# Fused attention and two feed-forward stages: the order of the first stage's tiles and block products on TensorE

## The chip, the cores and the metric

The kernel runs on one core of one Trainium2 chip. The metric is the device time of one execution in microseconds, the median over the runs shown. TensorE (PE) does the matrix products, its weight loads are a separate row (PEld), VectorE (DVE) and ScalarE (ACT) do elementwise work and are the only ones besides PE that reach PSUM here, GpSimd (POOL) and SyncE (SP) issue DMAs.

## What is computed

Banded attention over 2 batches of 8 heads, 576 positions of 64; its output is a matrix x of 1152 tokens by 512. Two feed-forward stages follow:

```python
p = domain_probs / (domain_probs.sum(-1, keepdims=True) + 1e-09)
for e in range(4):                          # w1[e]: 512 x 1024, w2[e]: 1024 x 512
    out += p[:, e:e + 1] * (np.maximum(x @ w1[e], 0.0) @ w2[e])
h = out @ w_in                              # 512 x 2048
g = (a0 + a1*h + a2*h*h + a3*h*h*h) / (1 + |b0|*|h| + |b1|*h*h + 1e-06)
return g @ w_out                            # 2048 x 512
```

The change is in the first of the two, the experts.

## The kernel before

**Tiling.** Tokens are cut into three chunks c of 384 and nine output tiles t of 128 (tile t lies in chunk t // 3). The 4096 hidden columns of the four experts are 16 units u of 256, and two units make a group g (expert g // 2), so there are eight groups. Every fp32 operand is split into a high and a low part, and a product of two such operands is three matmuls (high by high, high by low, low by high).

**Three kinds of work on PE.** `h_paced` (line 894) makes the hidden values of one unit for one chunk: 24 matmuls of 384 columns into a PSUM tile `ps_h` of two banks, then a Relu on ACT that writes the high part `hh` (line 481) and a DVE instruction for the low part `hl` (line 485). `strassen` (line 917) makes them for chunks 1 and 2 together, with seven block products in place of eight; each `product` is six matmuls of 384 columns (line 933). `o_paced` (line 904) makes an output tile of a group: twelve matmuls of 512 columns into a bank `ps_o` (line 509), which ACT scales into `part` (line 539) and POOL adds to `acc` in SBUF by an accumulating DMA (line 540). Products and hidden values are the 384-column work, output tiles the 512-column work.

**A block of seven products** holds two `ps_h` tiles. In `yz` the bank y is written by products 1, 6, 7 and 4, and z by product 2; in `vz` the bank v is written by 5 and 3, and q holds a sum. Product 1 goes to y, and ACT copies y to z (line 947). Product 6 (called with `s(0, 0), t_(0)`) adds to y, product 5 starts v, and ACT copies v to the SBUF tile `p5` (line 955). Then DVE writes v = y + p5 (line 956). Product 7 adds to y, and DVE writes q = y + p5 (line 940, in `add`). Product 2 adds to z, product 3 to v, product 4 to y. Relus of both tiles end the block.

**The order** is fixed in Python: `tc.manual_schedule()` keeps each engine's instructions as they are written. `later(wait, ...)` puts a DVE or ACT step into the program behind the first PE step that passes its due time, so the second add of a block (`add(q, y, p5)`) stands behind product 2. `settle(key)` forces pending steps of that name into the program. Weight splits, sums of weight blocks and a conversion of the second stage's weights fill DVE in between. Waits between engines are set by the framework from the tiles that instructions read and write.

**Output tiles among the rest.** The loop over groups (line 987) hands each `strassen` call three fills, one output tile each, run behind products 1, 5 and 2 (`then(0)` to `then(2)`). Two more places between the hidden values of chunk 0 take one tile and two. Tiles 0 to 2 of a group are done in its second block, the other six in the next group. `o_bank` rotates over two PSUM banks; `h_tile` rotates over three two-bank tiles.

Of the kernel before, what the change touches and what calls it, by code (L numbers as in the profile page):

```python
# [18 lines left out]
F32 = mybir.dt.float32  # L19
# [82 lines left out]
def body(ctx, tc, qkv, mask, dp, w1, w2, w1d, w2d, coef, out):  # L102
# [51 lines left out]
    def block_sums(raw):  # L154

        r = raw.rearrange("p (h k i f) -> p h i k f", h=2, k=2, i=2)
        a11, a12, a21, a22 = r[:, 0, 0], r[:, 1, 0], r[:, 0, 1], r[:, 1, 1]
        sums = (
            (a22, a21, a22, ALU.add), (a21, a11, a21, ALU.subtract),
            (a11, a22, a11, ALU.subtract), (a12, a12, a11, ALU.subtract),  # L160
        )
# [316 lines left out]

    def relu_parts(u, c, ps):
        def high():  # L480
            nc.scalar.activation(new_h(u, c)[0], ps[:, :, :TC], AF.Relu)  # L481
# [137 lines left out]
    with tc.manual_schedule():  # L619
# [271 lines left out]
                    then()  # L891
            behind(0.0, key, act_then(key, act, dve, COST["token"]))

        def h_paced(u, c):
            settle(("w1", u))
            ps = h_tile()
# [20 lines left out]
        def strassen(u, between_):  # L917

            for k in (("w1", u), ("sw", u, 0), ("sw", u, 1), "tokens"):
                if k != ("sw", u, 0) or u % 2 == 0:  # L920
                    if u > 2 or k[0] != "sw":
                        settle(k)
            yz, vz = h_tile(), h_tile()
            z, y, v, q = yz[:, 0, :TC], yz[:, 1, :TC], vz[:, 0, :TC], vz[:, 1, :TC]
            w = [i.rearrange("p (h k i f) -> p h i k f", h=2, k=2, i=2) for i in (w1s[u][:, 0], w1s[u][:, 1])]
            block = lambda m, h, i: [t[:, h, i] for t in m]
            x = lambda c, h: [t[:, 2 * h:2 * h + 2] for t in xt[c]]
            t_ = lambda n: [t[:, n] for t in tt]
            s = lambda h, i: [sw[u, i][:, n, h] for n in range(2)]
            def product(out, a, b, first=False):  # L930
# [8 lines left out]
            def add(out, a, b):  # L939
                later(0.2, COST["add"], ("add", u), lambda: nc.vector.tensor_tensor(out=out, in0=a, in1=b, op=ALU.add))  # L940

            def then(n):
                for f, *args in between_[n]:
                    f(*args)

            product(y, block(w, 0, 0), x(1, 0), first=True)
            nc.scalar.copy(z, y)
            then(0)
            settle(("sw", u, 0))
            product(y, s(0, 0), t_(0))  # L950
            settle("first")
            settle(("sw", u, 1))
            product(v, s(1, 1), x(2, 0), first=True)
            p5 = st.tile([128, TC], F32, tag="p5", name="p5")
            nc.scalar.copy(p5, v)
            later(0.8, COST["add"], ("add", u), lambda: nc.vector.tensor_tensor(out=v, in0=y, in1=p5, op=ALU.add))
            then(1)
            settle(("add", u))
            settle("second")
            product(y, s(0, 1), t_(1))  # L960
            add(q, y, p5)
            product(z, block(w, 1, 0), x(1, 1))
            then(2)
            settle(("add", u))
            product(v, s(1, 0), x(2, 1))
            settle("third")
            product(y, block(w, 1, 1), t_(2))
            for c, ps, wait in ((1, yz, 1.1), (2, vz, 2.0)):
                high, low = relu_parts(u, c, ps)
                high()  # L970
                later(wait, COST["relu"], ("h", u, c), low)

        def loads(*us):
            for load, u in us:
# [12 lines left out]
        for g in range(NG1):  # L987
# [3 lines left out]
            if g == 0:  # L991
                later(0.0, COST["osum"], ("o", 0, 3), lambda: o_sum(0, 3, ps_2[3]))
                token_sums()
                tokens_later(temp[0], *(t[:, 0] for t in tt))
                sums_later(2)
                sums_split_later(2, 0)
# [5 lines left out]
                sums_split_later(2, 1)  # L1002
# [4 lines left out]
            if g in BLOCKED:  # L1007
                if g > 1:
                    h_paced(u, 0)
                sums_split_later(u + 1, 1)  # L1010
                if g > 1:
                    split_later(w2s, "w2", u + 1)
                if again:
                    split_later(w1s, "w1", u + 2)
                if g > 1:
                    o_paced(g - 1, 6)
                    h_paced(u + 1, 0)
                if g > 1:
                    o_paced(g - 1, 7)
                    if again:  # L1020
                        o_paced(g - 1, 8)
                fills = [o((g - 1, j if g > 1 else j + 3)) for j in (3, 4, 5)]
                w2_loads = (load_w2, u + 2), (load_w2, u + 3)
                free = [(load_w1, u + 3)] * (g > 1) + [w2_loads[0]] * (g == 1) + [w2_loads[1]]
                free = [(weights_free, *free)] if again else []
                fills[2].insert(0, (sums_split_later, u + 1, 0, free))
                strassen(u, fills)
# [7 lines left out]
                strassen(u + 1, (o((g, 0)), o((g, 1)), o((g, 2) if again else (g - 1, 8))))  # L1035
                if g == 1:
                    Window.spare[:] = [None, lone[:, 0], lone[:, 1]]
                if again:
                    sums_split_later(u + 2, 0, [(loads, (load_w1, u + 4))])
                    sums_later(u + 3)  # L1040
                else:
                    loads(*w2_loads, (load_w1, u + 4), (load_w1, u + 5))

        while Pace.prep:
            run_prep()
# [8 lines left out]
        early_open, late = tc.tile_pool(name="early", bufs=1), []  # L1054
        early = early_open.__enter__()
        dt = [rat.tile([128, 3, 2, TC], F32R, tag=f"t{i}", name=f"t{i}", bufs=1) for i in range(2)]
        ps_h, ps_2, p5s, x2_ps, turned, copied, rational = {}, {}, {}, {}, set(), {}, {}
        tokens = lambda c, h: [t[:, 2 * h:2 * h + 2] for t in xt[c]]

# [81 lines left out]
        def product(n, u):  # L1141
# [3 lines left out]
            if n == 5:  # L1145
# [12 lines left out]
                5: lambda: (place(2, 0), summed(1, 1), tokens(2, 0)),  # L1158
                6: lambda: (place(1, 1), summed(0, 0), d(0)),
                7: lambda: (place(1, 1), summed(0, 1), d(1)),  # L1160
            }[n]()
            first = n in (1, 5)
            for k in range(2):
# [145 lines left out]
```

## Time and profile before

| | |
|---|---|
| median of 3 runs | 631.29 us (631.0 to 631.78) |
| profiled execution, its own time | 631.96 us |
| its span, first to last instruction | 630.2 us |
| PE busy | 622.2 us, 99% of the span |
| DVE, ACT, POOL busy | 522.8, 370.4, 87.7 us |
| granted TensorE clock | 1.000 (2.4 GHz) |
| chain that ended last | PE 97% |

Busy PE time overlaps itself, since matmuls are pipelined: two rows of 0.33 us stand 0.17 us apart. So the time of PE's work is read from starts, not from durations. The experts' stretch runs from about 110 to 413 us.

### The profile page before, as it was taken

The page shows a single profiled execution, that of the slowest core. Times are in us where ns is not written, and L with a number is a line of the kernel's source. Part 1 is how long each engine was busy: PE and PEld are TensorE (multiplying, and loading weights), DVE is VectorE, ACT ScalarE, POOL GpSimd, SP SyncE. Part 2 cuts the span into 40 slices and gives each one's busy share as a digit, 9 for nine tenths or more (in the row PEclk, how much of TensorE's full clock was granted, in tenths as well). Part 3 has the DMA queues.
Part 4 walks back from the last instruction along what each step waited for, and adds up shares of the span by engine and source line. Part 5 has one row for each costly group of instructions (what it writes and reads, how often), then busy time and mean ns, then how long its engine had stood idle before and what let it go on. Part 6 is the DMA issues. An engine that isn't in the chain of part 4 may idle for free.

```text
span 630.2 us, 9848 instructions
## 1 busy us (share of the span) xinstructions
PE 622.2 (99%) x3726; PEld 555.8 (88%) x3728; DVE 522.8 (83%) x788; ACT 370.4 (59%) x682; POOL 87.7 (14%) x103
## 2 busy tenths in 40 slices
PE   8999999999999999999999999999999999999997
PEld 5888898999999999998998999888998889899886
DVE  7687488898888888889798888549898999899894
ACT  6787624345545554554555554336688686887760
POOL 2223230012112112101102112000000011111100
PEclk9999999999999999999999999999999999999999
DMA  9945302269869869869869877681231563573333
GB/s 284 316 136 185 103 20 68 100 166 241 246 187 270 245 180 258 257 186 267 241 182 261 236 220 219 209 323 48 88 133 56 190 201 89 116 235 52 66 81 103
DMA packets 39535, 111.28 MB, mean 177 GB/s; under 512 B 4256, under 2 KB 5024, under 8 KB 37440
## 3 DMA queue, kind: packets, MB, share of 16 engines
q1 hardware_dynamic: 29104, 92.14, 43.2%
q0 software_dynamic: 9936, 18.09, 16.5%
q8 instruction: 29, 0.48, 0.3%
q10 hardware_dynamic: 448, 0.43, 0.3%
q14 instruction: 18, 0.15, 0.1%
HBM read 67.13 MB, written 25.43 MB: 147 GB/s over the span
## 4 chain that ended last, share of the span: by engine, by line
PE 97%; DVE 1%; ACT 1%; issue 0%; POOL 0%; POOLq 0%
PE ps_o L509 46%; PE ps_h L464 21%; PE ps_h L933 16%; PE ps_h L1165 7%; PE ps_v L428 2%; PE ps_s L414 1%; PE ps_h L509 1%; PE ps_s L359 1%; PE ps_h L651 1%; PE ps_h L1099 1%; ACT pr L393 0%; POOL pr L403 0%; PE ps L359 0%; DVE xl L889 0%; DVE hl L485 0%
## 5 line engine op out<-in xcount | busy, mean ns | idle before, releaser
L509 PE MATMUL ps_o<-w,hh 128*128 128x512 f32 (+1 forms) x848 | 229.5, 392 | 0.3 <-DVE xl L452 0.3
L509 PEld LDWEIGHTS ps_o<-w,hh 128*128 128x128 f32 x848 | 156.6, 188 | 28.4 <-DVE xl L452 0.7
L509 PE MATMUL ps_o<-w,hl 128*128 128x512 f32 (+1 forms) x424 | 131.4, 391 | 0.1
L464 PE MATMUL ps_h<-xh,w 128*128 128x384 f32 x464 | 125.2, 338 | 0.0
L509 PEld LDWEIGHTS ps_o<-w,hl 128*128 128x128 f32 x424 | 79.3, 188 | 18.0 <-DVE hl L485 0.6
L464 PEld LDWEIGHTS ps_h<-xh,w 128*128 128x128 f32 x464 | 84.4, 188 | 2.3 <-issue 1.2
L540 POOL DMA_DIRECT2D acc<-part x51 | 44.7, 876 | 275.7 <-ACT part L539 216.9
L539 ACT ACTIVATE part<-ps_o,p_sb 128x512 f32<-128x512 f32 x51 | 35.1, 689 | 78.5 <-PE ps_o L509 36.8
L464 PE MATMUL ps_h<-xl,w 128*128 128x384 f32 x232 | 77.6, 335 | 0.0
L481 ACT ACTIVATE hh<-ps_h 128x768 fp32r<-128x768 f32 x48 | 37.4, 810 | 34.6 <-PE ps_h L464 23.0
L485 DVE SCALAR_TENSOR_TENSOR hl<-ps_h,hh 128x768 fp32r<-128x768 f32 x48 | 44.5, 950 | 10.8 <-ACT hh L481 10.7
L464 PEld LDWEIGHTS ps_h<-xl,w 128*128 128x128 f32 x232 | 43.6, 188 | 0.6
L1084 POOL DMA_DIRECT2D acc<-part x18 | 15.6, 867 | 184.3 <-ACT part L1083 183.8
L933 PE MATMUL ps_h<-t,sw 128*128 128x384 f32 x168 | 34.3, 339 | 0.0
L829 DVE TENSOR_TENSOR w<-raw,w 128x512 fp32r<-128x512 f32 x48 | 32.8, 684 | 1.0 <-ACT w L825 0.9
L393 ACT ACTIVATE pr<-pr,mx 128x80 f32<-128x80 f32 (+1 forms) x84 | 29.8, 358 | 6.1 <-DVE mx L387 4.7
L933 PE MATMUL ps_h<-xh,sw 128*128 128x384 f32 x112 | 33.2, 337 | 0.0
L268 ACT ACTIVATE x<-x 128x512 f32<-128x512 f32 x32 | 21.8, 681 | 18.1 <-DVE t L265 12.3
L933 PEld LDWEIGHTS ps_h<-t,sw 128*128 128x128 f32 x168 | 30.3, 188 | 2.2
L576 DVE SCALAR_TENSOR_TENSOR sq<-sq,absb,ab 128x768 f32<-128x768 f32 x24 | 24.2, 1013 | 7.9 <-ACT sq L565 6.7
L933 PE MATMUL ps_h<-xh,w 128*128 128x384 f32 x104 | 30.7, 335 | 0.0
L825 ACT CAST w<-raw 128x512 fp32r<-128x512 f32 x48 | 28.0, 617 | 0.0
(157 smaller groups left out, 1120.0 us busy)
## 6 DMA issues: line engine op xcount, KB each, us to landing
acc<-part POOLq DMA_DIRECT2D x69, 256.0 KB, 4.4
raw<-in_w_dram SPq DMA_DIRECT2D x32, 512.0 KB, 5.0
w<-w SPq DMA_DIRECT2D x14, 1024.0 KB, 6.3
w<-lone SPq DMA_DIRECT2D x19, 512.0 KB, 4.2
x<-in_w1d_dram SPq DMA_DIRECT2D x16, 512.0 KB, 3.8
x<-in_w2d_dram SPq DMA_DIRECT2D x16, 512.0 KB, 5.0
w<-w SPq DMA_DIRECT2D x13, 512.0 KB, 4.4
sw<-sw SPq DMA_DIRECT2D x12, 512.0 KB, 7.5
```

Source lines behind the costliest of these rows:

```text
L393: nc.scalar.activation(pr[:, j, i], pr[:, j, i], AF.Exp, scale=-1.0, bias=self.mx[:, j, i:i + 1], accum_out=self.total[:, j, i:i + 1],)
L464: nc.tensor.matmul(ps[:, i, :TC], lhsT=a[:, k, f], rhs=b[:, k], start=k + n == 0, stop=k + n == 5,)
L481: nc.scalar.activation(new_h(u, c)[0], ps[:, :, :TC], AF.Relu)
L485: nc.vector.scalar_tensor_tensor(out=hl, in0=ps[:, :, :TC], scalar=0.0, in1=hh.bitcast(F32), op0=ALU.max, op1=ALU.subtract,)
L509: nc.tensor.matmul(ps, lhsT=a[:, i, tk], rhs=b[:, i, cols], start=v + n == 0, stop=v + n == 6)
L539: nc.scalar.activation(part, ps, AF.Copy, scale=pe)
L540: nc.gpsimd.dma_start(acc[t], part, accum_op=ALU.add)
L576: nc.vector.scalar_tensor_tensor(out=self.sq, in0=self.sq, scalar=absb[:, 1:2], in1=self.ab, op0=ALU.mult, op1=ALU.add,)
L825: nc.scalar.copy(store[u][:, 0, s_], raws[nm, u][:, s_])
L829: nc.vector.tensor_tensor(out=w[:, 1, s_], in0=raws[nm, u][:, s_], in1=w[:, 0, s_].bitcast(F32), op=ALU.subtract)
L933: nc.tensor.matmul(out, lhsT=a[i][:, k], rhs=b[j][:, k], start=first and k + n == 0, stop=k + n == 3, skip_group_check=not first,)
L1165: nc.tensor.matmul(out, lhsT=a[i][:, k], rhs=b[j][:, k], start=first and k + m == 0, stop=k + m == 3, skip_group_check=not first,)
```

## The change

The number of matmuls and of instructions on every other engine stays the same (DVE 784, ACT 601, SP 177, POOL 97 in both programs). The seven products become methods of a class `Blocks`, and the loop calls them in a new order: block `a` (first unit of the group) and block `b` (second) now overlap, and output tiles stand in three runs of three tiles per group (6 to 8 and 3 to 5 of the group before, 0 to 2 of its own). Product 5 is written to a bank of the output tiles and copied to `p5` from there, so a `vz` tile is taken only at the first sum. `h_tile` can be told whether to take the third tile. The sums of weight blocks are formed in another order, and the products' halves are renamed to suit; the second stage gets the same renaming. The third tile of some runs has its `part` step held back by 1.5 us.

```diff
-    def h_tile(count=[0]):
+    count = [0]
+    def h_tile(last=None):
         count[0] += 1
-        pool = third[0] if third and count[0] % 3 == 0 else psh
+        last = third and count[0] % 3 == 0 if last is None else last
+        pool = third[0] if last else psh
...
-        def o_paced(g, t):
+        def o_paced(g, t, wait=0.0):
...
             if by_dma(g, t):
-                o_sum(g, t, ps)
+                if wait:
+                    later(wait, 0.0, ("o", g, t), lambda: o_sum(g, t, ps))
+                else:
+                    o_sum(g, t, ps)
...
+            def add(self, n, wait=0.2):
+                out, y, p5 = self.place(n), self.place(1), self.p5
+                later(
+                    wait, COST["add"], ("add", self.u),
+                    lambda: nc.vector.tensor_tensor(out=out, in0=y, in1=p5, op=ALU.add),
+                )
...
+            def fifth(self):
+                settle("first")
+                ps = o_bank()[:, :TC]
+                self.product(ps, self.summed(0, 1), self.x(2, 0), first=True)
+                self.p5 = st.tile([128, TC], F32, tag="p5", name="p5")
+                nc.scalar.copy(self.p5, ps)
...
+            def seventh(self):
+                settle(("add", self.u))
+                self.product(self.place(1), self.summed(0, 0), self.t(1))
+                self.add(3)
+
+            def second(self):
+                self.product(self.place(0), self.plain(1, 0), self.x(1, 1))
+
+            def third(self):
+                settle(("add", self.u))
+                self.product(self.place(2), self.summed(1, 0), self.x(2, 1))
...
+                h_paced(u, 0, False)
...
+                run(g - 1, 6, 7, 8)
+                a.first(False)
+                h_paced(u + 1, 0, True)
+                a.fifth()
+                a.sixth()
+                a.sum_up(0.2, False)
+                run(g - 1, 3, 4)
+                sums_split_later(u + 1, 0, free)
+                o_paced(g - 1, 5, 1.5)
+                a.seventh()
+                a.second()
+            b.first(True)
+            a.third()
+            a.fourth()
+            next_sums()
+            b.fifth()
+            b.sixth()
+            b.sum_up(0.2, False)
+            run(g, *range(3 if again else 2))
+            b.seventh()
+            b.second()
+            b.third()
+            b.fourth()
```

Before, on PE, in the second block of group 3: the end of product 2 (adds to `ps_h_2354`, the block's `yz`), one output tile `ps_o_2447`, and the start of product 3 (adds to `ps_h_2355`, its `vz`):

```order
L933 MATMUL ps_h_2354<-xh1_119,w1_1996 128x384 x2
L933 MATMUL ps_h_2354<-xl1_120,w1_1996 128x384
L933 MATMUL ps_h_2354<-xh1_119,w1_1996 128x384
L509 MATMUL ps_o_2447<-w2_1971,hh_2083 128x512 [waits Activation_49]
L509 MATMUL ps_o_2447<-w2_1971,hh_2083 128x512 x3
L509 MATMUL ps_o_2447<-w2_1971,hl_2084 128x512 x2
L509 MATMUL ps_o_2447<-w2_2128,hh_2151 128x512 x4
L509 MATMUL ps_o_2447<-w2_2128,hl_2152 128x512 x2
L933 MATMUL ps_h_2355<-xh2_121,sw_2313 128x384 [waits DVE_49]
L933 MATMUL ps_h_2355<-xl2_122,sw_2313 128x384
```

Now, the same place, `yz` being `ps_h_2331` and `vz` `ps_h_2383`:

```order
L935 MATMUL ps_h_2331<-xh1_119,w1_2012 128x384 x2
L935 MATMUL ps_h_2331<-xl1_120,w1_2012 128x384
L935 MATMUL ps_h_2331<-xh1_119,w1_2012 128x384
L935 MATMUL ps_h_2383<-xh2_121,sw_2302 128x384 [waits DVE_49]
L935 MATMUL ps_h_2383<-xl2_122,sw_2302 128x384
L935 MATMUL ps_h_2383<-xh2_121,sw_2302 128x384 x2
L935 MATMUL ps_h_2383<-xl2_122,sw_2302 128x384
L935 MATMUL ps_h_2383<-xh2_121,sw_2302 128x384
```

Product 3 still waits for DVE, and the output tile that stood between products 2 and 3 is gone from there.

The DVE rows of that place now (`ps_h_2383<-ps_h_2331,p5` is the block's second add, and it waits for PE and for nothing else; in the program before, its row reads the same):

```order
L833 TENSOR_TENSOR w2_2425<-raw_2171,w2_2425 128x512
L285 TENSOR_SCALAR f_2455<-t_2430 128x512 [waits DVE_49]
L289 SCALAR_TENSOR_TENSOR f_2455<-x64_2299,f_2455 128x512 [waits DVE_49]
L961 TENSOR_TENSOR ps_h_2383<-ps_h_2331,p5_2374 128x384 [waits PE_49]
L833 TENSOR_TENSOR w1_2457<-raw_2310,w1_2457 128x512 [waits DMAHW3_49,Activation_49]
L298 TENSOR_TENSOR f_2455<-f_2455,t_2430 128x512 [waits DVE_49]
L311 SCALAR_TENSOR_TENSOR f_2455<-x64_2299,f_2455 128x512 [waits DVE_49]
L489 SCALAR_TENSOR_TENSOR hl_2488<-ps_h_2383,hh_2487 128x768 [waits Activation_49]
```

Between the add and the low part of the Relu (`hl`, L489) stand three instructions of weight work. In the two programs product 3 has a DVE wait, and this add is the last DVE instruction ahead of it that writes its tile.

Now, in the first block of group 3 (`yz` is `ps_h_2162`, `vz` `ps_h_2237`): the end of product 2, product 1 of the second block (into `ps_h_2331`), and product 3 of the first:

```order
L935 MATMUL ps_h_2162<-xh1_119,w1_1762 128x384
L935 MATMUL ps_h_2331<-xh1_119,w1_2012 128x384 [waits PE_49]
L935 MATMUL ps_h_2331<-xl1_120,w1_2012 128x384
L935 MATMUL ps_h_2331<-xh1_119,w1_2012 128x384 x2
L935 MATMUL ps_h_2331<-xl1_120,w1_2012 128x384
L935 MATMUL ps_h_2331<-xh1_119,w1_2012 128x384
L935 MATMUL ps_h_2237<-xh2_121,sw_2083 128x384 [waits DVE_49]
```

Before, an output tile stood there as in the second block; now one product of the other block does.

Counted in the two orders from output tile 4 of group 0 to the last tile of group 7, PE changes from products to output tiles 55 times before and 23 times now, with 726 matmuls of 512 columns and 870 of 384 in both.

## Rows read from the trace of the kernel before

**Rows 1.** The page: busy time of each engine, and the granted clock in 40 slices.

```profile
PE 622.2 (99%) x3726; PEld 555.8 (88%) x3728; DVE 522.8 (83%) x788; ACT 370.4 (59%) x682; POOL 87.7 (14%) x103
...
PEclk9999999999999999999999999999999999999999
```

**Rows 2.** PE's two longest waits: line, releaser, us in total, times, longest.

```profile
PE ps_h L651 <- DVE warm L641: 1.2, 1, 1.2
PE ps_s L414 <- POOL pr L403: 1.0, 1, 1.0
```

**Rows 3.** Two stretches of 48 us, by engine: busy us (x count), clock, DMA share, GB/s.

```profile
141.00:189.00 48.00, 48.00 (x243) 43.45 (x242) 41.37 (x72) 25.58 (x43) 7.80 (x9) 1.00 0.81 224
189.00:237.00 48.00, 48.00 (x242) 43.45 (x241) 41.98 (x74) 26.30 (x45) 7.82 (x9) 1.00 0.82 234
```

**Rows 4.** PE in time, two output tiles between products: start us, us, instruction, count.

```profile
231.01 1.09 PE L509 MATMUL ps_o<-w,hh 128*128 128x512 f32 x4
...
233.78 1.07 PE L509 MATMUL ps_o<-w,hh 128*128 128x512 f32 x4
...
236.50 0.33 PE L933 MATMUL ps_h<-xh,w 128*128 128x384 f32 x1
...
237.56 0.39 PE L509 MATMUL ps_o<-w,hh 128*128 128x512 f32 x1
```

**Rows 5.** PE in time, second block of group 3, from product 7 to product 4.

```profile
212.94 1.23 PE L933 MATMUL ps_h<-t,sw 128*128 128x384 f32 x6
...
214.87 0.33 PE L933 MATMUL ps_h<-xh,w 128*128 128x384 f32 x1
215.04 1.08 PE L509 MATMUL ps_o<-w,hh 128*128 128x512 f32 x4
...
217.80 0.33 PE L933 MATMUL ps_h<-xh,sw 128*128 128x384 f32 x1
...
218.87 1.20 PE L933 MATMUL ps_h<-t,w 128*128 128x384 f32 x6
219.91 0.33 PE L464 MATMUL ps_h<-xh,w 128*128 128x384 f32 x1
```

**Rows 6.** DVE in time: second adds (L940) of the second blocks of groups 2 and 3.

```profile
167.34 0.57 DVE L940 TENSOR_TENSOR ps_h<-ps_h,p 128x384 f32<-128x384 f32 x1 [1.41 <-PE ps_h L933]
...
215.24 0.57 DVE L940 TENSOR_TENSOR ps_h<-ps_h,p 128x384 f32<-128x384 f32 x1 [0.95 <-PE ps_h L933]
215.71 0.68 DVE L829 TENSOR_TENSOR w<-raw,w 128x512 fp32r<-128x512 f32 x1
```

**Rows 7.** All second adds (L940): count, ns min/median/max, first and last start; idle before.

```profile
L940 DVE TENSOR_TENSOR ps_h<-ps_h,p x14: 566/567/567, 103.8 to 404.1; 128x384 f32<-128x384 f32 x14
...
  PE ps_h L933: 17.0, 13
```

**Rows 8.** DVE, PEld and PE in time, where PE waited for a DVE result.

```profile
95.07 0.95 DVE L485 SCALAR_TENSOR_TENSOR hl<-ps_h,hh 128x768 fp32r<-128x768 f32 x1
...
96.07 0.30 PEld L509 LDWEIGHTS ps_o<-w,hl 128*128 128x128 f32 x2 [0.56 <-DVE hl L485]
96.08 0.73 PE L509 MATMUL ps_o<-w,hl 128*128 128x512 f32 x2
...
96.64 0.34 PE L933 MATMUL ps_h<-t,sw 128*128 128x384 f32 x1
```

**Rows 9.** The tile `part`: ACT's writes, ACT's waits for a landing, landing times.

```profile
L539 ACT ACTIVATE part<-ps_o,p_sb x51: 667/690/692, 131.2 to 406.9; 128x512 f32<-128x512 f32 x51
...
  ACT part L539: 3.1, 1
DMA to landing us min/median/max: 3.3/4.5/9.9
```

**Rows 10.** ACT in time: the copy of y to z (L947) and of v to `p5` (L955).

```profile
206.15 0.49 ACT L947 COPY ps_h<-ps_h 128x384 f32<-128x384 f32 x1
...
210.37 0.48 ACT L955 COPY p<-ps_h 128x384 f32<-128x384 f32 x1 [0.86 <-PE ps_h L933]
```

More of the change, by code (lines that the diff above doesn't have):

```diff
@@ L912, in o_paced, with __init__, place, product @@
             if by_dma(g, t):
-                o_sum(g, t, ps)
+                if wait:
+                    later(wait, 0.0, ("o", g, t), lambda: o_sum(g, t, ps))
+                else:
+                    o_sum(g, t, ps)
             else:
                 later(0.2, COST["osum"], ("o", g, t), lambda: o_sum(g, t, ps))
[L917 to L930, printed above, removed]
+        class Blocks:
+            def __init__(self, u):
+                self.u = u
+            def place(self, n):
+                return (self.yz if n < 2 else self.vz)[:, n % 2, :TC]
+            def product(self, out, a, b, first=False):
                 for k in range(2):
@@ L937, in product @@
                 passed(COST["p"])
[L939 to L969, printed above, removed]
-                high()
-                later(wait, COST["relu"], ("h", u, c), low)
+            def plain(self, h, i):
+                settle(("w1", self.u))
+                parts = (w1s[self.u][:, n].rearrange("p (h k i f) -> p h i k f", h=2, k=2, i=2) for n in range(2))
+                return [t[:, h, i] for t in parts]
@@ new lines, in summed, with x, t @@
+            def summed(self, h, i):
+                settle(("sw", self.u, i))
+                return [sw[self.u, i][:, n, h] for n in range(2)]
+            def x(self, c, h):
+                return [t[:, 2 * h:2 * h + 2] for t in xt[c]]
+            def t(self, n):
+                settle(("tokens", "second", "third")[n])
+                return [t[:, n] for t in tt]
+            def add(self, n, wait=0.2):
[4 more added lines that the diff above has]
+                )
@@ new lines, in relu, with first @@
+            def relu(self, c):
+                settle(("add", self.u))
+                high, low = relu_parts(self.u, c, self.yz if c == 1 else self.vz)
+                high()
+                later(1.1, COST["relu"], ("h", self.u, c), low)
+            def first(self, last=None):
+                settle("tokens")
+                self.yz = h_tile(last)
+                self.product(self.place(1), self.plain(0, 0), self.x(1, 0), first=True)
+                nc.scalar.copy(self.place(0), self.place(1))
@@ new lines, in fifth, with sixth, sum_up @@
+            def fifth(self):
[4 more added lines that the diff above has]
+                nc.scalar.copy(self.p5, ps)
+            def sixth(self):
+                self.product(self.place(1), self.summed(1, 1), self.t(0))
+            def sum_up(self, wait=0.2, last=None):
+                self.vz = h_tile(last)
+                self.add(2, wait)
@@ L1006, in body, with next_sums @@
                 continue
[L1007 to L1027, printed above, removed]
+            a, b = (Blocks(v) for v in (u, u + 1))
+            w2_loads = (load_w2, u + 2), (load_w2, u + 3)
+            free = [(load_w1, u + 3)] * (g > 1) + [w2_loads[0]] * (g == 1) + [w2_loads[1]]
+            free = [(weights_free, *free)] if again else []
+            run = lambda g, *ts: [o_paced(g, t, 1.5 * (n == 2)) for n, t in enumerate(ts)]
+            def next_sums():
                 if again:
@@ L1034, in body @@
                     loads((load_w1, u + 3))
-                strassen(u + 1, (o((g, 0)), o((g, 1)), o((g, 2) if again else (g - 1, 8))))
-                if g == 1:
-                    Window.spare[:] = [None, lone[:, 0], lone[:, 1]]
-                if again:
[L1039 to L1042, printed above, removed]
+            if g == 1:
+                sums_split_later(u + 1, 1)
+                split_later(w1s, "w1", u + 2)
+                a.first(False)
+                o_paced(0, 6)
+                a.sixth()
+                a.fifth()
+                a.sum_up(0.8, False)
+                o_paced(0, 7)
+                a.seventh()
+                a.second()
+                sums_split_later(u + 1, 0, free)
+                o_paced(0, 8)
+            else:
+                for v in (u, u + 1):
+                    new_h(v, 0)
+                h_paced(u, 0, False)
+                sums_split_later(u + 1, 1)
+                split_later(w2s, "w2", u + 1)
+                if again:
+                    split_later(w1s, "w1", u + 2)
+                run(g - 1, 6, 7, 8)
+                a.first(False)
+                h_paced(u + 1, 0, True)
+                a.fifth()
+                a.sixth()
+                a.sum_up(0.2, False)
+                run(g - 1, 3, 4)
+                sums_split_later(u + 1, 0, free)
+                o_paced(g - 1, 5, 1.5)
+                a.seventh()
+                a.second()
+            b.first(True)
[10 more added lines that the diff above has]
+            b.fourth()
+            if g == 1:
+                Window.spare[:] = [None, lone[:, 0], lone[:, 1]]
+            if again:
+                sums_split_later(u + 2, 0, [(loads, (load_w1, u + 4))])
+                sums_later(u + 3)
+            else:
+                loads(*w2_loads, (load_w1, u + 4), (load_w1, u + 5))
         while Pace.prep:
```

29 lines of the change are left out of this document (19 added, 10 removed).

## The prediction

> **What bounds the kernel now.** I read the page first: PE is busy for 99% of the span, DVE for 83%, and the clock never leaves its full level [rows 1]. So the question is whether PE has idle time to win or only work. The list of PE's waits answers it: the longest is 1.2 us, and both of those shown lie in attention, before the stretch that the change touches [rows 2]. The busy time by stretch says the same: in the experts' part PE is busy 48.00 of 48 us, twice, and DVE about 42 [rows 3]. No wait can be removed here. A gain can only come from PE doing the same matmuls closer together, and a loss from a wait that is new.
>
> The third view is PE in time. Of two output tiles in a row, the first takes 233.78 - 231.01 = 2.77 us, the second 236.50 - 233.78 = 2.72 us; the product between two tiles takes 237.56 - 236.50 = 1.06 us [rows 4], while one that follows a product takes 219.91 - 218.87 = 1.04 us [rows 5]. So going from products to tiles and back costs about 0.05 + 0.02 = 0.07 us. The period of a group confirms it: the second adds of two groups start 215.24 - 167.34 = 47.90 us apart [rows 6]. A group is 132 matmuls of 384 columns, 22 sixes of 1.04 us = 22.88 us, and nine tiles of 2.72 us = 24.48 us, together 47.36 us. The 0.54 us that are left, over eight round trips, are 0.068 us each.
>
> **The runs.** The two orders have 55 and 23 changes to output tiles, so 32 round trips go: 32 x 0.068 = 2.2 us. Bounds: nothing, if the price is not one of the change of kind; and 32 x 0.075 = 2.4 us, with the rows' rounding against me. I take 2.2, since two readings agree. This work is on the path, PE having no idle time.
>
> The Trainium skill, "TensorE: Matmul & The Clock Gate", section "Back-to-back issue gap", gives the start-to-start time of a matmul by its own columns alone, N / 2.4 + 2.5 ns, which is 216 and 163 ns. This trace has about 227 (2.72 us over twelve) and 173 ns (1.04 over six), and a first tile that is longer than the second; by the rule the number of runs would not matter and the saving would be nil.
>
> **The wait that is uncovered.** The second add of a block, q = y + p5, is placed behind product 2 in both programs. It does not start when product 7 has given y. In the second block of group 3 product 2 gives way to the next PE instruction at 215.04 [rows 5], and the add starts at 215.24, after DVE idled 0.95 us for PE [rows 6]. Thirteen of the fourteen adds were waited for like that, 17.0 us in all, and each takes 0.567 us [rows 7]. Product 3 in turn waits for a DVE result, and the last DVE write to its tile is this add, though that goes to the other bank. Before, an output tile of 2.76 us (217.80 - 215.04) [rows 5] stood between products 2 and 3, and the add was over by 215.81. The wait existed and cost nothing. In the second block of every group the change puts product 3 directly behind product 2. So PE must stand still:
>
> - 0.20 us from the end of product 2's slot to the start of the add (215.24 - 215.04);
> - 0.57 us for the add;
> - 0.06 us from the end of a DVE instruction to the matmul that waits for it: 95.07 + 0.95 = 96.02, the matmul starts at 96.08 [rows 8];
> - 0.11 us because that matmul's weights come late: the two matmuls from there take 96.64 - 96.08 = 0.56 us, two in steady flow 0.45 (a sixth of 2.72 us).
>
> That is 0.94 us, in seven groups 6.6 us. Bounds of one stall: 0.77 us if restart is free, and 1.05 us with twice the restart's 0.06 and a rounding more. Behind product 3 on PE's queue stand product 4 and the hidden values of the next group; ACT's Relus are late by as much, which costs nothing more, as PE is late too.
>
> The last 0.11 us is there because the weight load waited too: it began at 96.07, after DVE's end and after 0.56 us of idle [rows 8]. The Trainium skill, same page, section "Step-by-step: what each phase is for", says that PE pulls weight loads ahead of matmuls in flight. By that each stall would lose 0.11 us, and the forecast would be 634.9 us; the row speaks against it, so the 0.11 stays.
>
> **The first block of a group** has product 1 of the other block between its products 2 and 3, 1.04 us. The add is over 0.77 us after product 2's slot, its result reaches PE at 0.83, and the weights of product 3 would be wanted some 0.11 us before its start, at 0.93. It just fits, if DVE stands ready, as it did 13 times of 14 [rows 7]. If another DVE instruction has begun, up to 0.68 us [rows 6] are added. In the first group an output tile stands there still, so six groups x 0.6 = 3.6 us is the upper bound; I take nothing, by the 13 of 14.
>
> **Product 5 in an output bank.** The copy to `p5` takes 0.48 us as before [rows 10]. The bank is wanted again by the second tile of the run behind it: product 6 (1.04) and a tile (2.72) later. Covered; without that cover it would cost 0.5 us and some latency. In the same way y is copied to z in 0.49 us [rows 10], with at least a product of another block and product 5 (2.08 us) before product 6 wants y.
>
> **Three tiles in a row** share two `part` buffers. ACT writes one in 0.69 us, and a landing takes 4.5 us in the median, 9.9 at most [rows 9]; with about 1 us from ACT's start to the issue, a buffer is free 5.5 us later. The third tile's `part` comes two tiles, 5.44 us, behind the first, and where it is held back 1.5 us more, at 6.9. So in the median nothing waits; before, one wait of 3.1 us was all [rows 9]. A late landing blocks ACT, and behind `part` on its queue stands the copy of y to z, which product 6 wants about 4 us after the run. I take nothing and keep it as a rival.
>
> The other edits cost nothing: the sums of weight blocks are the same four DVE instructions in another order, the counts on DVE, ACT, SP and POOL are equal, POOL's order is the same, and SP's loads move by a few places while their readers move with them. DVE keeps 6 us spare in 48 [rows 3], which covers that.
>
> **The sum.** 6.6 - 2.2 = +4.4 us on the profiled execution's 631.96 us, so 636.4. The median of the runs is 0.67 us lower, 631.29, so I forecast **635.7 us**. A measurement of this kernel tells 0.2%, 1.3 us, from no change.
>
> **Rivals.**
>
> - *The add is free earlier* (10%). If it could start when product 7 ends, 1.04 us sooner, it would be over before product 3 is due: 0.20 + 0.57 + 0.06 is below 1.04. This decides the sign. Then only the 2.2 us remain: 629.1 us. Against it: the idle time before 13 of 14 adds, which a free y would not have left, and the start 0.20 us behind product 2.
> - *Runs have no price* (8%). The longer first tile could come from what runs beside it, and not from the change of kind. Then the stalls stand alone: 631.29 + 6.6 = 637.9 us. Against it: the period of a group gives the same price as single tiles. (The section "Back-to-back issue gap" of the Trainium skill's "TensorE: Matmul & The Clock Gate", above, is a rule by which it would come out so.)
> - *Bursts of adds to memory* (12%). DMA engines are already busy 0.81 of the time [rows 3], and three accumulating DMAs in a row may land later. A first landing of 9.9 us would put the buffer's return at 10.9 us, 5.5 us behind the third tile's end, and the copy of y to z behind it: 5.5 + 0.69 + 0.49 is 2.7 us past the 4 us that product 6 leaves. One such case in the program gives 638.4 us, two 641.1. For it: the wait of 3.1 us before; against it: a median with a margin.
> - *The stalls as reckoned* (70%).
>
> **The numbers.** My own case alone spans 7 x 0.77 - 2.4 = +3.0 to 7 x 1.05 - 1.6 = +5.8, 634.3 to 637.1 (1.6 if only a tile's 0.05 us is saved). To hold 8 in 10 the range takes in the runs without price and one late landing, and a little below the first bound: 633.3 to 638.9. Faster by more than 0.2% is the first rival, 0.10; within 0.2% needs the add to be half covered, 0.03; slower has the rest, 0.87.
>
> **What would show it.** Right: in the list of PE's waits a new row, `ps_h` waiting for DVE's add in the product's line, seven times about 0.9 us; in PE's time a gap ahead of product 3 in each second block; groups 47.90 + 0.94 - 5 x 0.068 = 48.5 us apart; output tiles of 2.77, 2.72 and 2.72 us in a run. Wrong: product 3 within 0.2 us of product 2, an add that starts before product 2 ends, or PE waits on ACT's `part`.

## The result: 0.75% slower, by a wait of 0.93 us in each of seven groups

The changed kernel took 635.96 us in the median of six runs (635.49 to 636.97), the kernel before 631.43 us (630.98 to 631.78, six runs). The ratio is 1.0075, 95% interval 1.0062 to 1.0088. The forecast was 635.7 us.

The first lines of the page of the changed kernel, and its chain of waits by engine:

```profile
span 635.0 us, 9851 instructions
...
PE 622.0 (98%) x3726; PEld 554.6 (87%) x3728; DVE 522.6 (82%) x788; ACT 371.5 (58%) x682; POOL 88.1 (14%) x103
...
PE 97%; DVE 1%; DMA 1%; ACT 0%; issue 0%
```

Beside [rows 1] no engine is busier by more than 1.1 us (ScalarE, 371.5 against 370.4): PE has the same 3726 matmuls and 622 us of work, spread over a span that is 4.8 us longer. The added time is idle time of PE. Its list of waits names it (line, releaser, us in total, times, longest), and the same row of the weight loads:

```profile
PE ps_h L935 <- DVE ps_h L961: 4.6, 7, 0.7
PE ps_s L362 <- DMA qk<-in_qkv_dram: 1.4, 1, 1.4
```

```profile
PEld ps_h L935 <- DVE ps_h L961: 7.0, 8, 1.0
```

Neither wait of [rows 2] stood in the experts' part; now the longest row is the block products' line (L935) waiting for VectorE's add (L961), seven times. The second row is a load at the start of attention, which the change doesn't touch.

The same two stretches as in [rows 3]:

```profile
141.00:189.00 48.00, 47.34 (x239) 42.69 (x238) 41.19 (x72) 27.40 (x46) 8.06 (x10) 1.00 0.83 234
189.00:237.00 48.00, 47.34 (x239) 42.69 (x238) 41.81 (x74) 25.32 (x42) 7.96 (x9) 1.00 0.81 227
```

PE is idle for 0.66 us in 48 by its busy time, where it was idle for none, at a full clock. Now the place itself, the second block of group 3: PE in time, from the last matmul of product 2, and DVE's add:

```profile
218.91 0.34 PE L935 MATMUL ps_h<-xh,w 128*128 128x384 f32 x1
219.90 0.44 PE L935 MATMUL ps_h<-xh,sw 128*128 128x384 f32 x1 [0.66 <-DVE ps_h L961]
220.18 0.34 PE L935 MATMUL ps_h<-xl,sw 128*128 128x384 f32 x1
220.36 0.51 PE L935 MATMUL ps_h<-xh,sw 128*128 128x384 f32 x2
```

```profile
170.76 0.57 DVE L961 TENSOR_TENSOR ps_h<-ps_h,p 128x384 f32<-128x384 f32 x1 [1.84 <-PE ps_h L935]
...
219.28 0.56 DVE L961 TENSOR_TENSOR ps_h<-ps_h,p 128x384 f32<-128x384 f32 x1 [0.67 <-PE ps_h L935]
```

A matmul of 384 columns follows the one before after 0.17 us. The first of product 3 follows after 219.90 - 218.91 = 0.99, the second after 0.28: 0.82 + 0.11 = 0.93 us lost. The add starts 0.20 us after product 2 would have given way (219.28 against 218.91 + 0.17), ends at 219.84, and PE goes on 0.06 later. The wait's own row says 0.66 us, because it counts from the end of the last matmul and not from its slot; the bill is read from starts. Two groups are 219.28 - 170.76 = 48.52 us apart.

### The profile page after: what moved, and what is told of

Same layout as the page of the kernel before. It is cut to its first block, busy times and chain, and to the rows that moved or that the text cites. A ratio compares the mean times of both kernels' runs of the same rounds, so it can differ in the third digit from the quotient of the medians.

```text
span 635.0 us, 9851 instructions
## 1 busy us (share of the span) xinstructions
PE 622.0 (98%) x3726; PEld 554.6 (87%) x3728; DVE 522.6 (82%) x788; ACT 371.5 (58%) x682; POOL 88.1 (14%) x103
## 4 chain that ended last, share of the span: by engine, by line
PE 97%; DVE 1%; DMA 1%; ACT 0%; issue 0%
PE ps_o L513 45%; PE ps_h L467 21%; PE ps_h L935 14%; PE ps_h L1232 7%; PE ps_o L935 2%; PE ps_v L431 2%; PE ps_s L417 1%; PE ps_h L513 1%; DMA qk<-in_qkv_dram 1%; PE ps_s L362 1%; PE ps_h L1166 1%; DVE ps_h L961 1%; PE ps_h L655 1%; PE ps L362 0%; DVE xl L893 0%
## 5 line engine op out<-in xcount | busy, mean ns | idle before, releaser
L485 ACT ACTIVATE hh<-ps_h 128x768 fp32r<-128x768 f32 x48 | 38.9, 812 | 41.0 <-PE ps_h L935 22.8
L489 DVE SCALAR_TENSOR_TENSOR hl<-ps_h,hh 128x768 fp32r<-128x768 f32 x48 | 45.4, 953 | 12.7 <-ACT hh L485 11.9
L935 PE MATMUL ps_h<-t,sw 128*128 128x384 f32 x168 | 34.0, 337 | 0.0
L935 PEld LDWEIGHTS ps_h<-t,sw 128*128 128x128 f32 x168 | 29.9, 188 | 1.2
L935 PE MATMUL ps_h<-xh,w 128*128 128x384 f32 x104 | 29.8, 336 | 0.0
L616 ACT CAST hh<-u 128x768 fp32r<-128x768 f32 x24 | 19.9, 838 | 13.4 <-DVE u L610 13.2
```

Of the source, the lines that this page charges most:

```text
L485: nc.scalar.activation(hh, ps[:, :, :TC], AF.Relu)
L489: nc.vector.scalar_tensor_tensor(out=hl, in0=ps[:, :, :TC], scalar=0.0, in1=hh.bitcast(F32), op0=ALU.max, op1=ALU.subtract,)
L935: nc.tensor.matmul(out, lhsT=a[i][:, k], rhs=b[j][:, k], start=first and k + n == 0, stop=k + n == 3, skip_group_check=not first,)
```

## Experiments

The kernel before ran beside each set on the same chip: 631.64 us (18 runs) with e1, e2, e3 and e7, 631.31 (7 runs) with e5, e6, e12 and e13, 631.28 (13 runs) with e15 and e17. Ratios are to that. The four medians of the kernel before lie between 631.28 and 631.64 us, so medians of different sets are compared below as they are.

**e1: cover for the second add.** Products 3 and 4 of the second block move behind the first hidden values of the next group. The last group has no next one; there an output tile stands between.

```
             b.seventh()
             b.second()
-            b.third()
-            b.fourth()
+            held[:] = b.third, b.fourth
...
                 h_paced(u, 0, False)
+                while held:
+                    held.pop(0)()
```

> Products 3 and 4 of a group's second block are moved behind the first hidden values of the next group (2.08 us of matmuls stand between products 2 and 3); in the last group one output tile stands there instead. Nothing is computed otherwise. Theory (uncovered add, and a price of 0.068 us for each run of output tiles): all seven waits of PE for the second add go, 6.5 us less than the changed kernel's 635.96, so 629.4 us; against the kernel before it keeps 31 saved round trips, -2.1 us. Rival A (runs have no price): the same waits go, but nothing is gained against before: 631.4 us. Rival B (the seven waits are only where lateness of other origin shows, such as bursts of accumulating DMAs on ACT): PE waits elsewhere, and the time stays above 633 us.

Measured: 629.79 us (628.6 to 630.76, seven runs), ratio 0.9963 [0.995, 0.9977]. No product waits for an add. VectorE's second adds of groups 2 and 3:

```profile
168.95 0.57 DVE L961 TENSOR_TENSOR ps_h<-ps_h,p 128x384 f32<-128x384 f32 x1 [1.83 <-PE ps_h L935]
...
216.51 0.57 DVE L961 TENSOR_TENSOR ps_h<-ps_h,p 128x384 f32<-128x384 f32 x1 [0.67 <-PE ps_h L935]
```

A group takes 47.56 us, 0.96 less than in the changed kernel with the same three runs a group. The runs of tiles are worth what was reckoned (0.34 us less than the 47.90 of [rows 6], for five runs fewer), and the wait is what hides it. One wait of another kind was left; ScalarE and PE in time:

```profile
361.63 0.69 ACT L543 ACTIVATE part<-ps_o,p_sb 128x512 f32<-128x512 f32 x1 [5.47 <-DMA acc<-part]
```

```profile
368.25 0.74 PE L513 MATMUL ps_o<-w,hl 128*128 128x512 f32 x2 [0.52 <-DVE hl L489]
```

ScalarE waited 5.47 us for an accumulating DMA to land; what stood behind it on its queue was late, the low half of h with it, and PE lost 0.69 + 0.11 us. That is the rival of the bursts, small and once in this execution.

**e2: one tile between.** The last tile of the second block's run goes between products 2 and 3, as cover; that makes 30 runs of tiles. The moved tile's copy is no longer held back.

```
-            run(g, *range(3 if again else 2))
+            run(g, *range(2 if again else 1))
             b.seventh()
             b.second()
+            o_paced(g, 2 if again else 1)
             b.third()
```

> The changed kernel with the last output tile of the run in the second block moved between products 2 and 3, as before the change; all else as in the changed kernel. Seven more runs (30 in place of 23). Theory: the seven waits go (-6.5 us) and seven round trips come back (+0.5 us): 635.96 - 6.0 = 629.9 us. Rival A (no price of runs): 631.4 less nothing, about 631.4 us. Rival B (lateness of other origin): above 633 us.

Measured: 628.86 us (628.7 to 629.91, four runs), ratio 0.9954 [0.9938, 0.997]: 2.8 us below the kernel before and 7 below the changed one. From 95 to 430 us PE has no wait at all. Two second adds:

```profile
165.54 0.57 DVE L961 TENSOR_TENSOR ps_h<-ps_h,p 128x384 f32<-128x384 f32 x1 [1.28 <-PE ps_h L935]
...
213.17 0.57 DVE L961 TENSOR_TENSOR ps_h<-ps_h,p 128x384 f32<-128x384 f32 x1 [1.80 <-PE ps_h L935]
```

A group takes 47.63 us. That is 0.07 more than in e1, for one run of tiles more in a group; against that it has no late copy that reaches PE, which cost e1 0.8 us in its profile.

Of the 2.8 us the 25 runs saved explain 1.7. The first add of the first block, in the kernel before and in e2, says where more of it lies:

```profile
99.53 0.55 DVE L956 TENSOR_TENSOR ps_h<-ps_h,p 128x384 f32<-128x384 f32 x1
```

```profile
98.08 0.56 DVE L961 TENSOR_TENSOR ps_h<-ps_h,p 128x384 f32<-128x384 f32 x1
```

In these two executions 1.45 us are won ahead of the reordered blocks (the changed kernel has this add at 99.67 us). Why is not shown, so only the 1.7 us belong to the order.

**e3: the price of a run alone.** As e1, with six runs of tiles in a group and not three (42 in all, 18 more).

```
-                run(g - 1, 6, 7, 8)
+                o_paced(g - 1, 6)
                 a.first(False)
+                o_paced(g - 1, 7)
                 h_paced(u + 1, 0, True)
+                o_paced(g - 1, 8)
```

(The second block's run of three is split into one tile and two, the first of them behind product 5.) The tiles that the edit takes out of a run of three also lose their hold-back of 1.5 us, so the price of a run is read from the period, not from the time.

> The kernel with products 3 and 4 behind the next group's hidden values, and its runs of three tiles cut up among products where no product needs them as cover: 42 runs of output tiles in place of 24, with the same matmuls. Theory: 18 round trips at 0.068 us are 1.2 us more than the kernel with 24 runs, so about 630.6 us, and the group's period is 0.2 us longer, with no wait of PE. Rival A (no price of runs): the same time and the same period as with 24 runs, within 0.1 us per group.

Measured: 632.09 us (630.41 to 635.22, twelve runs), ratio 1.0008 [0.9995, 1.0021]. The second adds of groups 2 and 3, and PE's one wait there:

```profile
168.97 0.57 DVE L961 TENSOR_TENSOR ps_h<-ps_h,p 128x384 f32<-128x384 f32 x1 [1.88 <-PE ps_h L935]
...
216.72 0.57 DVE L961 TENSOR_TENSOR ps_h<-ps_h,p 128x384 f32<-128x384 f32 x1 [0.66 <-PE ps_h L935]
```

```profile
PE ps_o L513 <- DVE hl L489: 1.6, 1, 1.6
```

A group takes 47.75 us. With no stall in it, a group of three, four, six and eight runs takes 47.56 (e1), 47.63 (e2), 47.75 (e3) and 47.90 us [rows 6]: (47.90 - 47.56) / 5 = 0.068 us for each, and 47.36 + n x 0.068 gives all four to 0.02 us. The time as a whole missed its forecast by 1.5 us, and PE did wait once: a late copy as in e1 costs it 1.6 us here. The spread of 4.8 us would fit such cases that come and go between runs; that is not shown, as one execution alone has a profile.

**e7: the add made to start early.** The second add is placed ahead of product 2 in the program, so that it waits for product 7 alone.

```
             b.seventh()
+            settle(("add", u + 1))
             b.second()
```

> In the second block the second add is put into the program ahead of product 2, so that it waits for product 7 alone. Theory (waits are set by whole tiles, and the add reads the tile that product 2 writes): product 2 now waits for the add in product 3's place; seven waits of 0.93 us remain, the total stays within 0.5 us of 635.96 us, and the row of PE's waits names the add ahead of product 2. Rival C (the wait is one of banks, and the add was only placed too late): product 2 writes the other bank and goes on, the add is over before product 3, and the time falls to about 629.4 us.

Measured: 637.31 us, one run, not a gain, and 1.35 us over the changed kernel where at most 0.5 was expected. PE's waits, and PE in time at the second block of group 3, products 7 and 2:

```profile
PE ps_h L935 <- DVE ps_h L961: 6.5, 7, 2.0
```

```profile
215.55 1.23 PE L935 MATMUL ps_h<-t,sw 128*128 128x384 f32 x6
217.72 0.44 PE L935 MATMUL ps_h<-xh,w 128*128 128x384 f32 x1 [0.94 <-DVE ps_h L961]
```

The wait has moved from product 3 to product 2. Four of the seven stalls have the length of the changed kernel's; in two VectorE was in another instruction when product 7 ended (0.3 us more), and in one the add stood behind an instruction that waited for a load of weights (1.3 us more). The add reads y in one half of the pair `yz`, product 2 writes z in the other half, and the wait is on the pair. So the rival by which the add is free when product 7 ends gives no gain: ahead of product 2 the add stops product 2, behind it the add stops product 3.

**e17: the same rule, from the other add.** In the second block product 2 goes ahead of product 7 and of the run.

```
-            run(g, *range(3 if again else 2))
-            b.seventh()
             b.second()
+            b.seventh()
+            run(g, *range(3 if again else 2))
             b.third()
```

> The changed kernel with another order in the second block: product 2 goes ahead of product 7 and of the run of three tiles, which then stands between products 7 and 3. By banks alone the first add (z before the seventh product) would be covered by product 2's 1.04 us against 0.83 us, the second add by three tiles, and PE would never wait: 629.4 us (the rival). Theory: waits go by the whole tile, whose two banks hold y and z; the first add then waits for product 2, as the second add does in the changed kernel, and product 7 waits 0.82 us for it, 7 times; 635.5 to 636.5 us, no gain over the changed kernel.

Measured: 635.79 us (635.55 and 636.04), ratio 1.0072 [1.0051, 1.0092]. PE in time around product 2, and VectorE's first add:

```profile
208.77 0.34 PE L935 MATMUL ps_h<-xh,w 128*128 128x384 f32 x1
209.82 1.32 PE L935 MATMUL ps_h<-t,sw 128*128 128x384 f32 x6 [0.71 <-DVE ps_h L961]
```

```profile
209.20 0.57 DVE L961 TENSOR_TENSOR ps_h<-ps_h,p 128x384 f32<-128x384 f32 x1 [0.75 <-PE ps_h L935]
```

y was ready a product earlier, but the add starts at 209.20, behind product 2, and product 7 loses 209.82 - 208.77 - 0.17 = 0.88 us, seven times. Work of the same pair is no cover for its add; only work that writes elsewhere is.

**e5: the fifth product in a bank of its own.** Undoes the part of the change that puts it into an output bank, in both blocks of a group.

```
-                ps = o_bank()[:, :TC]
+                self.vz = h_tile(False)
+                ps = self.place(2)
...
-                self.vz = h_tile(last)
```

> The change with one part undone: the second block's fifth product goes to a bank of its own pair again (the pair of h banks that the second block uses anyway), not to a bank of the output tiles. Theory (the borrowed bank is what lets the products stand in a row with no tile between them): the h pair is only free when the low half of the first block's Relu has been read out of it, so product 5 of the second block now waits for that on VectorE, some 1.6 to 2 us in each of 7 groups, on top of the 7 waits of 0.93 us for the second add; time 645 to 650 us, with a new wait row of the product line on hl or ps_h of 10 us and more in total. Rival (the bank is of no account, some h pair is free by then): 635.5 to 636.5 us, PE's waits as in the changed kernel.

Measured: 646.52 us (646.08 and 646.97), ratio 1.0235 [1.0209, 1.0261]. PE's two longest waits, and the place of the new one:

```profile
PE ps_h L935 <- DVE hl L489: 8.7, 7, 1.6
PE ps_h L935 <- DVE ps_h L961: 4.6, 7, 0.7
```

```profile
210.60 0.44 PE L935 MATMUL ps_h<-xh,sw 128*128 128x384 f32 x1 [1.43 <-DVE hl L489]
```

The old seven waits stay as they were, and seven new ones come, product 5 of the second block for the low half of the first block's Relu. Second adds of the second blocks at 223.30 and 273.55 make a group of 50.25 us, 1.7 more than the changed kernel's. So the borrowed bank is needed by the new order, and in the changed kernel's list no product and no tile waits for it.

**e6: without the hold-back.** The changed kernel has ScalarE's copy of a run's third tile placed 1.5 us later; here it isn't.

```
-            run = lambda g, *ts: [o_paced(g, t, 1.5 * (n == 2)) for n, t in enumerate(ts)]
+            run = lambda g, *ts: [o_paced(g, t) for n, t in enumerate(ts)]
...
-                o_paced(g - 1, 5, 1.5)
+                o_paced(g - 1, 5)
```

> The change without the 1.5 us by which it holds back ScalarE's copy of the third tile of a run. Theory (only the wait for the second add makes the change slower): the 7 waits of 0.93 us stand, the period of a group stays 48.5 us, time 635.3 to 636.6 us. Rival (runs of three send accumulating transfers in bursts, and the hold-back is what spreads them): ScalarE's waits for landings grow beyond the 14.5 us of the changed kernel, a copy of the low half of h comes late, PE waits for it, and the time is over 637.5 us.

Measured: 641.59 us (640.24 to 642.14, four runs), ratio 1.0153 [1.0133, 1.0174]. My theory missed by 5 us. The rival held in the time and in the landing waits (22.6 us in place of 14.5); what came late was another step than the one it named. The second block of group 5, in turn on ScalarE, on VectorE and on PE:

```profile
318.48 0.69 ACT L543 ACTIVATE part<-ps_o,p_sb 128x512 f32<-128x512 f32 x1 [4.49 <-DMA acc<-part]
319.07 0.61 ACT L241 CAST w<-f 128x512 fp32r<-128x512 f32 x1
```

```profile
319.71 0.69 DVE L245 TENSOR_TENSOR w<-f,w 128x512 fp32r<-128x512 f32 x1 [3.62 <-ACT w L241]
320.32 0.56 DVE L961 TENSOR_TENSOR ps_h<-ps_h,p 128x384 f32<-128x384 f32 x1
```

```profile
316.68 0.34 PE L935 MATMUL ps_h<-xh,w 128*128 128x384 f32 x1
320.93 0.69 PE L935 MATMUL ps_h<-xh,sw 128*128 128x384 f32 x1 [3.91 <-DVE ps_h L961]
```

ScalarE's third copy waits 4.49 us for a landing; a weight conversion behind it is late; VectorE waits for that 3.62 us; and the second add stands behind VectorE's waiting instruction, though its own operand was long there. Product 3 comes 320.93 - 316.68 = 4.25 us after the matmul before. Behind that pause PE runs at half speed, by stretches:

```profile
308.00:316.00 8.00, 8.00 (x39) 6.82 (x38) 7.04 (x14) 3.44 (x6) 1.76 (x2) 1.00 0.77 231
...
321.00:324.00 3.00, 3.00 (x10) 3.00 (x11) 1.50 (x3) 0.75 (x1) 0.00 (x0) 0.50 0.98 262
```

The granted clock was 1.00 before and 0.50 in the 3 us after it (1.2 GHz, the lower level). By starts, this place costs 3.3 us of waiting more than a stall of the changed kernel, and 1.5 us of slower matmuls. Two more stalls add 1.7 us: 0.6 at 155.65 us, ahead of product 3 of a first block, and 1.1 at 269.16 us, where the second add stands behind a VectorE instruction that waits for a load of weights. Whether these two come from the hold-back is not shown.

**e15: without the hold-back, but covered.** e2 with the edit of e6.

> As e2 (one tile between the second block's products 2 and 3), and as e6 without the 1.5 us hold-back of the third copy. Theory, formed after e6 (there ScalarE's copy waited for a landing, VectorE's conversion behind it, the second add behind that, and PE waited because the add has no cover): with 2.77 us of tile between product 2 and product 3 the same lateness finds cover, so PE's waits stay under 2 us in total although ScalarE again waits 18 us or more for landings; time 628.5 to 630 us. Rival (without the hold-back late copies reach PE by other ways too, through hl or the banks of the output tiles): PE waits 3 us or more, time over 632 us.

Measured: 630.03 us (629.78 to 630.98, ten runs), ratio 0.998 [0.9971, 0.999]. ScalarE's waits for landings from 110 to 415 us, in e6:

```profile
ACT part L543 <- DMA acc<-part: 22.6, 9, 5.5
```

In e15, PE's waits for adds from 95 to 430 us, and ScalarE's for landings:

```profile
PE ps_h L935 <- DVE ps_h L961: 0.2, 1, 0.2
```

```profile
ACT part L543 <- DMA acc<-part: 16.0, 6, 3.7
```

ScalarE still waits 16.0 us for landings, less than the 18 expected and with a longest wait of 3.7 us against e6's 5.5, so the lateness is not quite the same. No second block waits. What reaches PE are two adds of first blocks, where a single product is the cover: by starts 0.3 us at 201.87 and 0.5 at 297.66.

```profile
297.08 0.34 PE L935 MATMUL ps_h<-xh,w 128*128 128x384 f32 x1
297.66 0.44 PE L935 MATMUL ps_h<-xh,sw 128*128 128x384 f32 x1 [0.24 <-DVE ps_h L961]
```

The edit that costs 5.6 us in the changed kernel (641.59 against 635.96) costs 1.2 where a tile covers the add (630.03 against 628.86). So most of what lateness costs in the changed kernel it costs because the add has no slack.

**e12 and e13: the third tile's sum on VectorE.** e1 and e2 with this edit. With it the sums that come out are no longer the same, for a reason that is not known, so the times are no times of this computation and only the waits are read:

```
-        return (1, 3) <= (g, t) < (NG1 - 1, 0)
+        return (1, 3) <= (g, t) < (NG1 - 1, 0) and t % 3 < 2
```

> As e1 (third and fourth products of the second block behind the next group's h), but the third tile of every run is added to its sum by VectorE straight from the bank, as tiles outside the DMA stretch are; ScalarE copies and accumulating transfers are left for the first two alone. Theory (in e1, what is left over above the 629.4 us reckoned, and its spread of 2.2 us between runs, come from ScalarE's copy waiting for the landing of the transfer two before it, 14.4 us in 6 waits, one of which reached PE): the landing waits fall below 5 us in total, no product or tile of PE waits for hl, the period stays at 47.56 us, time 628.6 to 629.4 us, spread under 1 us. Rival (VectorE, 0.69 us more per such tile, becomes late): PE waits for second adds or for hl again, 7 times 0.3 us and more, time over 630.5 us.

> As e2 (one tile between the second block's products 2 and 3), with the third tile of every run added by VectorE instead of by an accumulating transfer. In e2 no wait for a landing reached PE, so theory: no change beyond 0.5 us from e2's 628.86, period 47.63 us, no PE wait in the groups. Rival (VectorE becomes late by 0.69 us per tile): PE waits for the second add or for hl, time over 630 us. A gain of more than 0.5 us would say that landings still cost e2 something that its profile doesn't show.

Measured: 653.61 us (ratio 1.0341 [1.032, 1.0361]) and 653.72 us (1.0356 [1.0333, 1.0379]). Both theories missed the total. PE's longest wait in e12:

```profile
PE ps_h L1176 <- DVE acc L546: 22.9, 1, 22.9
```

It lies past the groups, at 433 us, where a transpose waits for a sum that came late on VectorE; from 110 to 400 us PE has no wait in e12, and ScalarE none for a landing from 110 to 390. In e13 the wait past the groups is 20.1 us, and PE waits twice within them (0.5 and 0.2 us), where none was expected. So without the third DMA of a run e12 has no landing wait and no late copy, but neither version can be used as it stands. How e1 would end with that mended wasn't tried.

## Why the prediction was right

- **What bounds.** PE had no wait to lose there; the added time shows as new idle time of PE alone, 0.66 us in 48.
- **The runs.** Reckoned at 0.068 us each, 2.2 us in all. By the four periods of e3's section it is 0.068. They differ by the number of changes between kinds at equal columns, so the rival that had no price falls. The Trainium skill, "TensorE: Matmul & The Clock Gate", section "Back-to-back issue gap", gives the gap of a single matmul by its own columns alone and says that in a stream the weight loads set it too. Columns and loads are the same in the four orders, so by that rule their periods would be equal. In the run ahead of the place shown above the tiles start at 208.77, 211.53 and 214.25 and the product behind them at 216.97, so they took 2.76, 2.72 and 2.72 us; 2.77, 2.72 and 2.72 were foretold.
- **The uncovered wait.** Reckoned at 0.20 + 0.57 + 0.06 + 0.11 = 0.94 us; measured 0.93 from starts, 0.96 by the period against e1. Seven of them, as said. e1 and e2 take them away with the runs left almost as they are, and the time falls below before's.
- **The weights that come late.** In each of the seven stalls the second matmul follows after 0.28 us and not 0.17, so the 0.11 us was right. That it would arise here at all was luck, since the row behind it could not tell: the load in [rows 8] fetches `hl` (line 509 has the hidden values as its weights), which is VectorE's result itself, so it could not have begun sooner. In the changed kernel the load fetches `sw`, of which product 7 had used another part, and it waits all the same:

```profile
218.74 0.19 PEld L935 LDWEIGHTS ps_h<-xh,w 128*128 128x128 f32 x1
219.90 0.19 PEld L935 LDWEIGHTS ps_h<-xh,sw 128*128 128x128 f32 x1 [0.98 <-DVE ps_h L961]
```

  The trace has the wait for VectorE's semaphore on this load and none on the matmul behind it, in all seven stalls; in the whole trace 352 loads have a wait of their own and no matmul has one. The Trainium skill's section "Step-by-step: what each phase is for", in the same page, has loads pulled ahead of matmuls in flight. The load that came late is the one that has the wait, here as in [rows 8], so neither place bears that out or speaks against it, though the prediction took [rows 8] to speak against it.
- **The first block of a group.** Taken at nothing. One of six didn't fit, at 398.71 us: VectorE was in a longer instruction of weight work (1.22 us) until its add, and PE lost 0.15 us. It is the eighth wait in the weight loads' row. With no more than one product as cover, this place had little slack: in e15 it lost up to 0.5 us.
- **Product 5.** No wait of PE for its bank stands in the list, and the order couldn't do without it (e5).
- **The bursts.** Their size was right for this kernel, none of them reaching PE, but the ground I gave was wrong: "in the median nothing waits". ScalarE waited for landings 14.5 us in five places, against 3.1 in one [rows 9], and the landing's median rose from 4.5 to 6.0 us:

```profile
ACT part L543 <- DMA acc<-part: 14.5, 5, 5.3
```

```profile
DMA to landing us min/median/max: 3.3/6.0/8.8
```

  In this kernel the 1.5 us hold-back matters, which the prediction names and does not price (e6: 5.6 us more without it). And it named the copy of y to z as what would be late; in e6 it was a weight conversion and the add behind it, in e1 and e3 the low half of h. That the term of nothing came out was in part luck.
- **The sum.** +4.4 us forecast, +4.5 between the medians (635.96 - 631.43); a group of 48.5 us foretold, 48.52 measured. The wait and the runs came out as reckoned, each by itself.

## What to carry over

A wait that costs nothing is held by the work that stands before it, so before work is pulled together for a price of 0.07 us a piece, look at which waits it covered: with one tile of 2.7 us left in its place the same change is 0.46% faster than the kernel before (0.27% by the runs saved), and without it 0.75% slower. Count cover only by work that writes other tiles than the waiting pair. Look, too, at what stands ahead on the releasing engine's queue: with no slack left, lateness there came through to the bound engine, as e6 and e7 show. A new order is costed from starts in the trace, not from the wait's own row, which leaves out a third of it.

## What was not expected of the hardware

Three accumulating DMAs close together landed in 6.0 us in the median and not in 4.5, with the DMA engines no busier (0.81 to 0.83 of the time in the stretches of [rows 3], in both kernels). In both traces those issued less than 4 us behind another landed later: 5.7 us in the median before (11 of them) and 6.7 now (24), the others 4.5 and 4.8. That closeness alone does it is not shown: e17, with the same runs, has a median of 4.9 us over all. A pause of PE of 4.2 us was followed by 3 us at a granted clock of 0.50, in which a matmul of 384 columns took 0.32 us and not 0.17: about 1.5 us more, so this stall cost a third more than its length. That is one case. Behind the stall of 1.9 us in the same execution the matmuls kept their 0.17 us, and the seven stalls of 0.93 us in the changed kernel left the clock at 1.00.
